# Padding the low part of q and the last value block to 128 rows in a causal attention, mixture-of-experts and dense kernel

## The chip, the cores and the metric

The kernel runs on one core of a Trainium2 chip. The metric is the device time of one execution in microseconds (us). In the profile PE is TensorE's matmul, PEld TensorE's weight load, DVE is VectorE, ACT ScalarE, POOL GpSimd and SP SyncE, which here issues DMAs.

## The reference

Four batches of eight heads (S = 576 positions, D = 64) go through causal attention with a compressive memory; the result, 2304 rows of 512, goes through a top-1 mixture of eight experts and then through a dense layer with a squared ReLU:

```python
scores = np.where(causal, -1000000000.0, scale * np.matmul(q, k.transpose(0, 1, 3, 2)))
a = np.exp(scores - scores.max(-1, keepdims=True))
a /= a.sum(-1, keepdims=True) + 1e-09
local = np.matmul(a, v)
...
x = _moe_ref(x=x, **moe_kwargs)
return _moe2_ref(x=x, **moe2_kwargs)
```

All of it is in float32.

## The kernel before

The attention works on pairs of heads: 16 pairs (b, hp), two heads side by side on 64 partitions each. For precision q/8 and k are each split into a high part in the matmul's own format (qh, kh) and a low part (ql, kl), and a score is qh·kh + qh·kl + ql·kh. For all pairs but the first, the first two products are one matmul with a contraction of 128 rows: SyncE copies, by eight DMAs a pair, qh twice and kh above kl into q2 and k2 (lines 201 and 202). The third product, `product(ql, kh, False, False)` in line 238, takes the 64 partitions of one head, and so its weight load and its matmul stand in the profile as 64\*128 (rows\*columns of the array). After it the causal mask is added by a 128-row matmul with the identity (line 239). `scores` is called for query blocks (3,), then (1, 0), then (2,); each call does both heads one after the other. The last 64 queries of both heads go through `psl` (lines 81 to 83, then 255), whose weights qlast are already 128 rows with zeros (POOL fills them from qh and ql).

A score block is reduced to its negated maximum (DVE, line 244), exponentiated (ACT, line 247), transposed (PE, line 77) and copied to aT (line 159). The product with the values (line 332, pva; line 337, pvb) puts the two heads on 64 columns each (128\*64); its last key block has only LAST = 64 keys and is 64\*64. The result is copied to pvs, transposed (ppt), scaled (DVE, line 350) and joined with the memory's part (POOL, xb).

A pair is a generator that is advanced in four lanes (prep, front, back, end), so that at any time one pair is prepared while another has its scores and a third its product with the values. Inside the attention a scheduler sets each engine's order; the engines then run their lists in order. The pools give each tile its buffers (`bufs`): qh, ql, k2, q2 had two, so a buffer is written again two pairs later. After the attention come the experts (lines 800 on) and the dense layer, in an order written out by hand.

Of the kernel before, what the change touches and what calls it, by code (L numbers as in the profile page):

```python
# [9 lines left out]
F32 = mybir.dt.float32  # L10
F32R = mybir.dt.float32r
# [9 lines left out]
P = 128  # L21
B, H, S, D = 4, 8, 576, 64
# [3 lines left out]
NB = 5  # L26
LAST = S - 4 * P
# [34 lines left out]
NPLAIN = 1  # L62
XB = 2
WARM = 11
MASK_LAST = True
TK = 3
TW = 0
PW = 6
# [67 lines left out]
def attention(tc, c, q, k, v, x_dram, pools):  # L136
    nc = tc.nc
    fr, ld, wk, aw, at, per, lt = pools
# [6 lines left out]
    qpad = [per.tile([P, SP_], F32, name=f"qpad{i}") for i in range(3)]  # L145
    pvs = [lt.tile([P, SP_], F32, name=f"pvs{i}") if i else per.tile([P, SP_], F32, name=f"pvs{i}") for i in range(2)]
    qlast = [[per.tile([P, P], F32R, name=f"qlast{t}{i}") for t in "hl"] for i in range(2)]
    for i in range(3):
        nc.gpsimd.memset(qpad[i][:, S:], 0.0)
    for i in range(2):  # L150
        nc.gpsimd.memset(pvs[i][:, S:], 0.0)
        for t in range(2):
            nc.gpsimd.memset(qlast[i][t].bitcast(F32), 0.0)
    c.setup()
    c.lg = c.pool.tile([P, NCOL, 2 * E], F32, name="lg")
    nc.gpsimd.memset(c.lg, 0.0)
# [4 lines left out]
    def pair(b, hp, lgT):  # L161
        i = (b * (H // 2) + hp) % 2
# [12 lines left out]
        kh = fr.tile([P, S], F32R, tag="kh", name="kh")  # L175
# [2 lines left out]
        early = nc.gpsimd if b or hp > 1 else nc.vector  # L178
        (nc.vector if EV["kl"] == "v" else early).tensor_sub(kl, ks, kh.bitcast(F32))
        yield  # L180
        qh = fr.tile([P, S], F32R, tag="qh", name="qh")
        ql = fr.tile([P, S], F32R, tag="ql", name="ql")
        ex = fr.tile([P, S], F32, tag="ex", name="ex", bufs=1)
        rq = fr.tile([P, S], F32, tag="rq", name="rq", bufs=1)
        nc.scalar.mul(qh, qs, 0.125)
        nc.scalar.activation(ex, qs, AF.Exp)
        nc.scalar.activation(rq, qs, AF.Relu)
        nc.vector.scalar_tensor_tensor(out=ql, in0=qs, scalar=0.125, in1=qh.bitcast(F32), op0=ALU.mult, op1=ALU.subtract)
        for t, src in enumerate((qh, ql)):
            for h in range(2):  # L190
                r = slice(64 * h, 64 * h + 64)
                early.tensor_copy(qlast[i][t][r, r], src[r, 512:S].bitcast(F32))
        stacked = b or hp >= NPLAIN
        if stacked:
            k2 = fr.tile([P, 2, 512], F32R, tag="k2", name="k2")
            q2 = fr.tile([P, 2, 512], F32R, tag="q2", name="q2")
            for h in range(2):
                r = slice(64 * h, 64 * h + 64)
                for g, (kx, n) in enumerate(((kh, 512), (kl, 512))):
                    o = slice(64 * g, 64 * g + 64)  # L200
# [4 lines left out]
            memory_consts(tc, c, per, *c.memory)  # L205
        yield "prep"

        vt = ld.tile([P, NB, 2, D], F32, tag="vraw", name="vraw", bufs=2)
        nc.sync.dma_start(out=vt[:, 0:4].rearrange("p c h d -> p c (h d)"), in_=v[b, hp, 0:512].rearrange("(c p) d -> p c d", p=P))
        nc.sync.dma_start(out=vt[0:LAST, 4].rearrange("p h d -> p (h d)"), in_=v[b, hp, 512:S])  # L210
        negm = wk.tile([P, 2, NB], F32, tag="negm", name="negm")
# [5 lines left out]
        def scores(js):  # L217
            banks = [bank(f"sc{js[0]}{h}") for h in range(2)]
            off = [sum((i + 1) * P for i in js[:t]) for t in range(len(js))]
            o, n = off[-1] + js[-1] * P, len(js)  # L220
            mask = c.maskd.unsqueeze(1).to_broadcast((P, n, P))
            for h in range(2):
                r = slice(64 * h, 64 * h + 64)

                def product(qx, kx, start, stop):
                    for i, j in enumerate(js):
                        nk = (j + 1) * P
                        lhs, rhs = (qx[:, h], kx[:, h]) if len(qx.shape) == 3 else (qx[r], kx[r])
                        nc.tensor.matmul(banks[h][:, off[i]:off[i] + nk], lhsT=lhs[:, j * P:nk], rhs=rhs[:, 0:nk],
                                         start=start and i == 0, stop=stop and i == n - 1)  # L230

                if stacked:
                    product(q2, k2, True, False)
                else:
                    product(qh, kh, True, False)
                    product(qh, kl, False, False)
                if MASK_LAST:
                    product(ql, kh, False, False)
                nc.tensor.matmul(banks[h][:, o - (n - 1) * P:o + P], lhsT=c.identb, rhs=mask, start=False, stop=MASK_LAST)  # L239
                if not MASK_LAST:  # L240
                    product(ql, kh, False, True)
            views = [(banks[h][:, off[i]:off[i] + (j + 1) * P], h, j) for i, j in enumerate(js) for h in range(2)]
            for psv, h, j in views:
                nc.vector.tensor_reduce(out=negm[:, h, j:j + 1], in_=psv, axis=AX.X, op=ALU.max, negate=True)  # L244
            for psv, h, j in views:
                nk = (j + 1) * P
                nc.scalar.activation(a[:, h, aoff[j]:aoff[j] + nk], psv, AF.Exp, bias=negm[:, h, j:j + 1],  # L247
                                     accum_out=ssum[:, h, j:j + 1])
# [10 lines left out]
        nc.gpsimd.tensor_copy(ssum[0:64, 1, 4:5], ssum[64:128, 0, 4:5])  # L259
        yield  # L260
        scores((3,))
        yield
        scores((1, 0))
        yield
        scores((2,))
        yield "front"

        aT = at.tile([P, 2, 1664], F32, tag="aT", name="aT", bufs=2)
        ko = (0, 576, 1024, 1344, 1536)

        def atr(dst, h, kb, j):
# [5 lines left out]
        for k0 in (0, 2):  # L277
            o, st = ko[k0 + 1] - 64, ko[k0 + 2] - ko[k0 + 1]
# [35 lines left out]
        for j0, j1 in ((0, 3), (3, 5)):  # L314
            pm = bank(f"pm{j0}")
            n = j1 - j0
            for j in range(j0, j1):
                nc.tensor.matmul(pm[:, (j - j0) * 130:(j - j0 + 1) * 130], lhsT=qpad[i3][:, j * P:(j + 1) * P], rhs=mb,
                                 start=True, stop=True)
# [5 lines left out]

        pa, pb = bank("pva"), bank("pvb")
        for kb in range(NB):
            kn = P if kb < 4 else LAST
            q0 = max(P, kb * P)
            for h in range(2):  # L330
                o = slice(64 * h, 64 * h + 64)
                nc.tensor.matmul(pa[o, q0 - P:448], lhsT=vt[0:kn, kb, h, :], rhs=aT[0:kn, h, ko[kb] + q0 - kb * P:ko[kb] + S - kb * P],
                                 start=(kb == 0), stop=(kb == NB - 1))
            if kb == 0:
                for h in range(2):
                    o = slice(64 * h, 64 * h + 64)
                    nc.tensor.matmul(pb[o, 0:P], lhsT=vt[:, 0, h, :], rhs=aT[:, h, 0:P], start=True, stop=True)
# [5 lines left out]
        for j0, j1 in ((0, 4), (4, 5)):  # L343
            n = j1 - j0
# [18 lines left out]
        for j0, j1 in ((0, 4), (4, 5)):  # L363
# [3 lines left out]
            n = P if j0 == 0 else 32  # L367
# [41 lines left out]

    order = list(pairs())  # L410
    gens = [pair(*o) for o in order]
    n = len(gens)

# [802 lines left out]
def body(tc, q, k, v, M, z, beta, wg, w1, w2, w_in, w_out, out, dbg=None):  # L1216
# [3 lines left out]
    with ExitStack() as top:  # L1220
# [18 lines left out]
        with ExitStack() as st:  # L1239
            e = st.enter_context  # L1240
            fr = e(tc.tile_pool(name="fr", bufs=2, reuse_waits="tile"))
            aw = e(tc.tile_pool(name="aw", bufs=2, reuse_waits="tile"))
            at = e(tc.tile_pool(name="at", bufs=2, reuse_waits="tile"))
            wk = e(tc.tile_pool(name="wk", bufs=2, reuse_waits="tile"))
            ld = e(tc.tile_pool(name="ld", bufs=4, reuse_waits="tile"))
            per = e(tc.tile_pool(name="per", bufs=1, reuse_waits="tile"))
            c.setup = lambda: (consts(tc, c, per, beta), route_consts(tc, c, rt, x_dram))
            c.memory = (wg, M, z)
            c.route = lambda b: route_batch(tc, c, b, rt)
            c.route_early = route_early(tc, c, cpool, rt)  # L1250
            with tc.manual_schedule(engines=AMAN) if AMAN else nullcontext():
                tail = attention(tc, c, q, k, v, x_dram, (fr, ld, wk, aw, at, per, lt))
            if dbg == "attn":
                for _ in tail:
                    pass
                nc.sync.dma_start(out=out, in_=x_dram[0:N, 0:DM])
                return
# [57 lines left out]
```

## Time and profile before

| what | value |
|---|---|
| median of 3 runs (lowest, highest) | 974.2 us (973.51, 974.49) |
| the profiled execution's own time | 973.51 us |
| its span, first to last instruction | 971.8 us |
| mean granted TensorE clock | 0.986 of full speed |
| PE, DVE, ACT busy over the span | 96%, 62%, 48% |

The profiled execution is the fastest of the three; 1.7 us lie outside its span. A busy PE is not PE at its peak: a matmul counts as busy from its issue to its modelled end, so time in which the array fills or empties is inside the busy time. The attention takes about the first 250 us, the experts up to about 640 us, the dense layer the rest, with the dense weights converted between.

### The profile page before, as it was taken

The numbers are of one execution on the slowest core, as the hardware profiler recorded it, in microseconds if no ns is written. First come the engines' busy times: TensorE is split into PE (matmuls) and PEld (weight loads), VectorE is DVE, ScalarE is ACT, GpSimd is POOL, SyncE is SP. The second block draws the span as 40 slices with busy tenths as digits, with TensorE's granted clock in tenths as the row PEclk, the third lists the DMA queues.
The fourth block names the chain that finished last, engine by engine and source line by source line (L and its number), as shares of the span: only waits on it lengthen the run. The fifth ranks groups of instructions, "written<-read, shape, count | busy, mean of one in ns | idle before, by whom it ended". The sixth has DMA issues, their size and how long they took to land. (4 is left out here: it accounts for less than half of the span.)

```text
span 971.8 us, 14590 instructions
## 1 busy us (share of the span) xinstructions
PE 930.1 (96%) x5212; PEld 735.4 (76%) x5212; DVE 599.5 (62%) x1142; ACT 468.7 (48%) x950; POOL 246.4 (25%) x301
## 2 busy tenths in 40 slices
PE   7999999999999999999999787799999999999996
PEld 4676676776566889889898565678888888888895
DVE  6677878778486887767678899943223222322232
ACT  6877777774445666565563444442222222322231
POOL 6233233231201033054322555562001100100010
PEclk8999999999999999999999999899999999999999
DMA  9675575552746978765735444431000100100000
GB/s 194 168 173 144 145 174 147 131 136 84 236 140 209 377 263 306 258 230 198 272 111 166 136 132 131 130 87 65 12 11 33 33 1 0 44 1 1 12 33 22
DMA packets 80923, 125.03 MB, mean 129 GB/s; under 512 B 8848, under 2 KB 35472, under 8 KB 80848
## 3 DMA queue, kind: packets, MB, share of 16 engines
q1 hardware_dynamic: 76224, 109.11, 37.1%
q0 software_dynamic: 4624, 14.95, 4.8%
q8 instruction: 43, 0.70, 0.3%
q14 instruction: 32, 0.26, 0.1%
HBM read 109.10 MB, written 15.99 MB: 129 GB/s over the span
## 5 line engine op out<-in xcount | busy, mean ns | idle before, releaser
L1165 DVE SCALAR_TENSOR_TENSOR r<-phf,r 128x512 f32<-128x512 f32 (+1 forms) x80 | 50.9, 636 | 178.9 <-ACT r L1164 178.9
L81 PE MATMUL phf<-yT,wi 128*128 128x512 f32 (+1 forms) x320 | 123.3, 385 | 19.2 <-DVE r L1165 19.2
L1164 ACT ACTIVATE r<-phf 128x512 f32<-128x512 f32 (+1 forms) x80 | 44.4, 555 | 177.9 <-PE phf L83 163.0
L848 DVE TENSOR_TENSOR wc<-raw,wc 128x1024 fp32r<-128x1024 f32 x91 | 117.3, 1331 | 12.0 <-ACT wc L846 10.3
L83 PE MATMUL phf<-yT,wi 128*128 128x512 f32 (+1 forms) x320 | 120.1, 375 | 0.0
L82 PE MATMUL phf<-yT,wi 128*128 128x512 f32 (+1 forms) x320 | 119.9, 375 | 0.0
L846 ACT CAST wc<-raw 128x1024 fp32r<-128x1024 f32 x108 | 106.5, 1056 | 20.0 <-DMA raw<-in_w_dram 14.8
L81 PE MATMUL po<-wo,gT 128*128 128x512 f32 x256 | 101.6, 398 | 1.5 <-ACT gT L1167 1.5
L82 PE MATMUL po<-wo,gT 128*128 128x512 f32 x256 | 101.0, 395 | 0.0
L83 PE MATMUL po<-wo,gT 128*128 128x512 f32 x256 | 89.0, 390 | 0.0
L81 PEld LDWEIGHTS phf<-yT,wi 128*128 128x128 f32 x320 | 61.2, 191 | 35.6 <-DVE r L1165 18.6
L244 DVE TENSOR_REDUCE negm<-sc 128x1 f32<-128x512 f32 (+3 forms) x128 | 59.0, 483 | 30.6 <-PE sc L239 28.6
L247 ACT ACTIVATE a<-sc,negm 128x512 f32<-128x512 f32 (+3 forms) x128 | 67.1, 529 | 21.5 <-DVE negm L244 20.7
L81 PE MATMUL py<-wc,hT 128*128 128x512 f32 x176 | 69.9, 397 | 0.7 <-ACT hT L885 0.7
L82 PE MATMUL py<-wc,hT 128*128 128x512 f32 x176 | 68.8, 391 | 0.8 <-DVE wc L848 0.8
L83 PEld LDWEIGHTS phf<-yT,wi 128*128 128x128 f32 x320 | 61.3, 192 | 10.8
L83 PE MATMUL py<-wc,hT 128*128 128x512 f32 x176 | 68.9, 391 | 0.3 <-DVE hT L886 0.3
L82 PEld LDWEIGHTS phf<-yT,wi 128*128 128x128 f32 x320 | 61.5, 192 | 10.0
L848 POOL TENSOR_TENSOR wc<-raw,wc 128x1024 fp32r<-128x1024 f32 x17 | 45.2, 2658 | 91.6 <-ACT wc L846 83.9
L1212 POOL DMA_INDIRECT out_dram<-ob,rtok x13 | 12.9, 991 | 204.7 <-DVE ob L1211 179.6
L1167 ACT CAST gT<-r 128x512 fp32r<-128x512 f32 x64 | 39.8, 621 | 45.4 <-DVE r L1165 37.0
L81 PEld LDWEIGHTS po<-wo,gT 128*128 128x128 f32 x256 | 49.3, 193 | 12.9 <-ACT gT L1167 2.2
(338 smaller groups left out, 2092.5 us busy)
## 6 DMA issues: line engine op xcount, KB each, us to landing
raw<-in_w_dram SPq DMA_DIRECT2D x64, 1024.0 KB, 6.7
fraw<-in_w_in_dram SPq DMA_DIRECT2D x16, 512.0 KB, 4.0
fraw<-in_w_out_dram SPq DMA_DIRECT2D x16, 512.0 KB, 3.7
q<-qh SPq DMA_DIRECT2D x60, 128.0 KB, 2.5
kraw<-in_k_dram SPq DMA_DIRECT2D x16, 288.0 KB, 5.3
qraw<-in_q_dram SPq DMA_DIRECT2D x16, 288.0 KB, 3.2
y_rest<-y SPq DMA_DIRECT2D x17, 256.0 KB, 3.0
vraw<-in_v_dram SPq DMA_DIRECT2D x16, 256.0 KB, 3.1
```

Of the source, the lines that this page charges most:

```text
L81: nc.tensor.matmul(out, lhsT=lh, rhs=rh, start=start, stop=False)
L82: nc.tensor.matmul(out, lhsT=lh, rhs=rl, start=False, stop=False)
L83: return nc.tensor.matmul(out, lhsT=ll, rhs=rh, start=False, stop=stop)
L244: nc.vector.tensor_reduce(out=negm[:, h, j:j + 1], in_=psv, axis=AX.X, op=ALU.max, negate=True)
L247: nc.scalar.activation(a[:, h, aoff[j]:aoff[j] + nk], psv, AF.Exp, bias=negm[:, h, j:j + 1], accum_out=ssum[:, h, j:j + 1])
L846: nc.scalar.copy(wc[:, 0, ks], raw[:, ks])
L848: eng.tensor_sub(wc[:, 1, ks], raw[:, ks], wc[:, 0, ks].bitcast(F32))
L1164: nc.scalar.activation(r[:, 0:nt], ph[:, 0:nt], AF.Relu)
L1165: nc.vector.scalar_tensor_tensor(out=r[:, 0:nt], in0=ph[:, 0:nt], scalar=0.0, in1=r[:, 0:nt], op0=ALU.max, op1=ALU.mult)
L1167: nc.scalar.copy(gT[:, 0, 0:nt], r[:, 0:nt])
L1212: nc.gpsimd.indirect_dma_start(out=out, out_offset=bass.IndirectOffsetOnAxis(ap=c.tok[b0 + j], axis=0), in_=ob, in_offset=None)
```

## The change

The low part of q gets a tile of its own, qlz, of 128 partitions and two head slots; in each slot only one head's 64 partitions are filled, by one DMA a head (two a pair), and the other 64 are zeroed once at the start. The third product takes these 128 rows against all 128 partitions of kh. The mask matmul now always ends the accumulation. The values and aT live in fixed tiles (vts, aTs, two of each) whose last block's rows 64 to 127 are zeroed once, and the product with the values uses 128 rows for the last block too. qh and ql go from two buffers to one.

```diff
+    qlz = [per.tile([P, 2, 512], F32R, name=f"qlz{i}") for i in range(2)]
+    vts = [per.tile([P, NB, 2, D], F32, name=f"vts{i}") for i in range(2)]
+    aTs = [per.tile([P, 2, 1664], F32, name=f"aTs{i}") for i in range(2)]
...
+        for h in range(2):
+            nc.gpsimd.memset(qlz[i][64 - 64 * h:128 - 64 * h, h].bitcast(F32), 0.0)
+        nc.gpsimd.memset(vts[i][LAST:P, 4], 0.0)
+        nc.gpsimd.memset(aTs[i][LAST:P, :, 1536:1600], 0.0)
...
-        qh = fr.tile([P, S], F32R, tag="qh", name="qh")
-        ql = fr.tile([P, S], F32R, tag="ql", name="ql")
+        qh = fr.tile([P, S], F32R, tag="qh", name="qh", bufs=1)
+        ql = fr.tile([P, S], F32R, tag="ql", name="ql", bufs=1)
...
-        for t, src in enumerate((qh, ql)):
-            for h in range(2):
-                r = slice(64 * h, 64 * h + 64)
+        for h in range(2):
+            r = slice(64 * h, 64 * h + 64)
+            nc.sync.dma_start(out=qlz[i][r, h].bitcast(F32), in_=ql[r, 0:512].bitcast(F32))
+            for t, src in enumerate((qh, ql)):
                 early.tensor_copy(qlast[i][t][r, r], src[r, 512:S].bitcast(F32))
...
-        vt = ld.tile([P, NB, 2, D], F32, tag="vraw", name="vraw", bufs=2)
+        vt = vts[i]
...
-                if MASK_LAST:
-                    product(ql, kh, False, False)
-                nc.tensor.matmul(banks[h][:, o - (n - 1) * P:o + P], lhsT=c.identb, rhs=mask, start=False, stop=MASK_LAST)
-                if not MASK_LAST:
-                    product(ql, kh, False, True)
+                for i_, j in enumerate(js):
+                    nk = (j + 1) * P
+                    nc.tensor.matmul(banks[h][:, off[i_]:off[i_] + nk], lhsT=qlz[i][:, h, j * P:nk], rhs=kh[:, 0:nk], start=False, stop=False)
+                nc.tensor.matmul(banks[h][:, o - (n - 1) * P:o + P], lhsT=c.identb, rhs=mask, start=False, stop=True)
...
-        aT = at.tile([P, 2, 1664], F32, tag="aT", name="aT", bufs=2)
+        aT = aTs[i]
...
-            kn = P if kb < 4 else LAST
...
-                nc.tensor.matmul(pa[o, q0 - P:448], lhsT=vt[0:kn, kb, h, :], rhs=aT[0:kn, h, ko[kb] + q0 - kb * P:ko[kb] + S - kb * P],
+                nc.tensor.matmul(pa[o, q0 - P:448], lhsT=vt[:, kb, h, :], rhs=aT[:, h, ko[kb] + q0 - kb * P:ko[kb] + S - kb * P],
```

On PE, in the middle of the attention, the end of one pair's product with the values and the next pair's scores of query block 2 stand like this in the kernel before (sc is the score bank of a head, k and q are the stacked tiles):

```order
L332 MATMUL pva<-aT,vraw 64x192 x2
L337 MATMUL pvb<-aT,vraw 64x128 x2
L332 MATMUL pva<-aT,vraw 64x64 x2
L229 MATMUL sc_1956<-k_1631,q_1632 128x384
L229 MATMUL sc_1956<-kh,ql 128x384
L239 LDWEIGHTS identb
L239 MATMUL sc_1956<-maskd,identb 128x128
```

The same place after the change:

```order
L337 MATMUL pva<-aTs_129,vts_127 64x192 x2
L342 MATMUL pvb<-aTs_129,vts_127 64x128 x2
L337 MATMUL pva<-aTs_129,vts_127 64x64 x2
L236 MATMUL sc_1973<-k_1648,q_1649 128x384
L246 MATMUL sc_1973<-kh,qlz_124 128x384
L247 LDWEIGHTS identb
L247 MATMUL sc_1973<-maskd,identb 128x128
```

No matmul is added or taken away and the order is the same; only the operands of the third product and of the last value block differ.

On SP, one pair's copies in the kernel before, from its loads of the values to the next pair's loads (the numbers tell the buffers of different pairs apart):

```order
L209 DMA vraw_1802<-in_v_dram 128x4x128
L210 DMA vraw_1802<-in_v_dram 64x128
L202 DMA q2_1834<-qh_1821 64x512
L201 DMA k2_1833<-kh_1798 64x512
L202 DMA q2_1834<-qh_1821 64x512
L201 DMA k2_1833<-kl_1800 64x512
L201 DMA k2_1833<-kh_1798 64x512
L202 DMA q2_1834<-qh_1821 64x512
L201 DMA k2_1833<-kl_1800 64x512
L202 DMA q2_1834<-qh_1821 64x512
L360 DMA x_dram_60<-xb_1772 128x4x128
```

And after the change, one pair's copies:

```order
L217 DMA vts1_127<-in_v_dram 64x128
L197 DMA qlz0_124<-ql_2039 64x512 x2
L208 DMA k2_2052<-kh_2016 64x512
L209 DMA q2_2053<-qh_2038 64x512
L208 DMA k2_2052<-kl_2018 64x512
L209 DMA q2_2053<-qh_2038 64x512
L208 DMA k2_2052<-kh_2016 64x512
L209 DMA q2_2053<-qh_2038 64x512
L208 DMA k2_2052<-kl_2018 64x512
L209 DMA q2_2053<-qh_2038 64x512
L365 DMA x_dram_60<-xb_1991 128x4x128
```

The two new copies stand ahead of the eight.

On ACT, the place around the copy of pva in the kernel before; kh_2000 belongs to the pair that is prepared next:

```order
L185 ACTIVATE qh_2225<-qraw_2200 128x576
L186 ACTIVATE ex_2227<-qraw_2200 128x576
L187 ACTIVATE rq_2228<-qraw_2200 128x576
L159 COPY pvs1_119<-pva_1940 128x448
L176 CAST kh_2000<-kraw_1996 128x576
```

The same place after the change, where kh_2016 is that pair's:

```order
L191 ACTIVATE qh_2038<-qraw_2014 128x576
L192 ACTIVATE ex_2242<-qraw_2216 128x576
L193 ACTIVATE rq_2243<-qraw_2216 128x576
L165 COPY pvs1_119<-pva_1957 128x448
L182 CAST kh_2016<-kraw_2012 128x576
```

Before, qh was written for the pair after the one whose kh follows; now qh and kh there belong to the same pair, and ex and rq run one pair ahead of qh.

## Rows read from the trace of the kernel before

**Rows 1.** The page's head: span, then busy time, share, and instructions of each engine.

```profile
span 971.8 us, 14590 instructions
...
PE 930.1 (96%) x5212; PEld 735.4 (76%) x5212; DVE 599.5 (62%) x1142; ACT 468.7 (48%) x950; POOL 246.4 (25%) x301
```

**Rows 2.** Windows: stretch, length, busy PE, PEld, DVE, ACT, POOL; clock, DMA share, GB/s.

```profile
131.70:146.00 14.30, 14.30 (x107) 10.26 (x106) 10.54 (x27) 10.85 (x33) 4.20 (x9) 1.00 0.68 181
...
160.10:175.70 15.60, 15.60 (x119) 11.27 (x118) 14.57 (x49) 10.55 (x28) 4.62 (x9) 1.00 0.64 169
218.50:233.60 15.10, 15.10 (x115) 10.69 (x114) 13.80 (x58) 7.83 (x25) 2.45 (x3) 1.00 0.15 41
233.60:245.50 11.90, 11.29 (x116) 8.19 (x115) 9.67 (x41) 5.47 (x17) 3.75 (x4) 1.00 0.56 198
```

**Rows 3.** Timeline of PE in one pair: start, duration, what, [idle before].

```profile
134.73 0.44 PE L229 MATMUL sc<-k,q 128*128 128x384 f32 x1
135.10 0.44 PE L229 MATMUL sc<-kh,ql 64*128 64x384 f32 x1
...
135.52 0.42 PE L229 MATMUL sc<-k,q 128*128 128x384 f32 x1
...
138.67 0.48 PE L229 MATMUL sc<-k,q 128*128 128x512 f32 x1
139.08 0.49 PE L229 MATMUL sc<-kh,ql 64*128 64x512 f32 x1
...
139.54 0.38 PE L82 MATMUL psl<-kl,qlasth 128*128 128x288 f32 x1
...
142.31 0.43 PE L229 MATMUL sc<-k,q 128*128 128x256 f32 x2
...
143.08 0.42 PE L229 MATMUL sc<-k,q 128*128 128x256 f32 x2
```

**Rows 4.** Timeline of PE's weight loads in the same pair.

```profile
134.47 0.19 PEld L332 LDWEIGHTS pva<-aT,vraw 64*64 64x64 f32 x4 [0.17 <-issue]
...
136.81 0.53 PEld L77 LDWEIGHTS ppt<-ident,pvs 128*128 128x128 f32 x5 [0.25 <-issue]
...
139.08 0.18 PEld L229 LDWEIGHTS sc<-kh,ql 64*128 64x128 f32 x1 [0.25 <-issue]
```

**Rows 5.** Groups by shape, weight loads, 0 to 420 us: busy, mean ns, idle before.

```profile
L229 PEld LDWEIGHTS sc<-kh,ql 64*128 64x128 f32 x128 | 21.3, 184 | 15.8 <-issue 13.1
...
L239 PEld LDWEIGHTS <-identb 128*128 128x128 bf16 x96 | 9.2, 95 | 16.2 <-issue 13.7
```

**Rows 6.** Timeline of PE in the experts, 128-row matmuls in a run.

```profile
349.90 0.39 PE L81 MATMUL py<-wc,hT 128*128 128x512 f32 x1
350.13 0.39 PE L82 MATMUL py<-wc,hT 128*128 128x512 f32 x1
```

**Rows 7.** Timeline of SP's queue in the pair of rows 3.

```profile
134.84 0.38 SPq L209 DMA_DIRECT2D vraw<-in_v_dram  x1
...
139.10 0.60 SPq L201 DMA_DIRECT2D k<-kh  x1
139.74 0.60 SPq L202 DMA_DIRECT2D q<-qh  x1
...
141.20 0.58 SPq L202 DMA_DIRECT2D q<-qh  x1
```

**Rows 8.** The page's DMA issues: count, KB each, median us from issue to landing.

```profile
q<-qh SPq DMA_DIRECT2D x60, 128.0 KB, 2.5
kraw<-in_k_dram SPq DMA_DIRECT2D x16, 288.0 KB, 5.3
```

**Rows 9.** Timeline of ACT around the copy of pva in that pair.

```profile
133.21 0.68 ACT L185 ACTIVATE qh<-qraw 128x576 fp32r<-128x576 f32 x1 [0.41 <-DMA qraw<-in_q_dram]
...
134.95 0.51 ACT L159 COPY pvs<-pva 128x448 f32<-128x448 f32 x1
```

**Rows 10.** Timeline of PE at the start of the attention.

```profile
17.85 1.11 PE L77 MATMUL ptl<-ident,al 128*128 128x128 f32 x4 [5.86 <-ACT al L257]
```

More of the change, by code (lines that the diff above doesn't have):

```diff
@@ L64 @@
 WARM = 11
-MASK_LAST = True
 TK = 3
```

## The prediction

> **What bounds the kernel now.** I read the page's head first: PE is busy for 96% of the span, no other engine above 62% [rows 1]. That share alone settles nothing, because a matmul that waits for the array counts as busy too, so I went to the attention, the only stage the change touches, and cut it at the starts of pva. There are fifteen stretches from one pair's pva to the next. Eleven are like the first of [rows 2], 14.3 us; in these PE is never idle, while DVE works 10.5 us and ACT 10.9. Two are like the second, 15.6 us, where a batch's routing brings DVE to 14.6. The last two rows are the last two stretches, 15.1 and 11.9 us. PE is thus the bound in the eleven, by more than 3 us, and DVE stands close behind it in the others.
>
> What PE does with its time shows when one follows the starts, not the durations. In the experts, 512-column matmuls of 128 rows start 0.23 us apart, though each is shown as 0.39 long [rows 6]. In the scores, the 512-column product of k and q starts at 138.67, the 64-row product with ql at 139.08, 0.41 later, and what stands behind the mask at 139.54 [rows 3]. Nothing waits for data there; the weight load of the 64-row product simply starts 0.25 us after the one before it ended, and "issue" names no releaser [rows 4]. The next weight load, of the mask's identity, idles too. Summed over the attention, PEld was idle 15.8 us ahead of the loads for ql and 16.2 us ahead of the identity's [rows 5]: 32.0 us, 2.0 a pair. So the array does not load the next weights beside a running matmul when the number of rows changes between the two. That is what I take the stall to be; the 128-row neighbours in [rows 6] don't have it.
>
> **The change, part by part.** *The third product at 128 rows.* It takes as many columns as before, so it costs no more streaming. In the order of the changed kernel the scores hold no switch of rows any more, save four at the start, where the first pair's first two products stay at 64 rows. I price it by starts. A head of block 2 (384 columns) takes 135.52 - 134.73 = 0.79 us [rows 3]; without a switch, at 0.23 us per 512 columns [rows 6], two products of 0.17 and a mask of 128 columns at 0.06 make 0.40. That saves 0.39, and 0.78 for two heads. Block 3 takes 0.87 [rows 3] and would take 0.23 + 0.23 + 0.06 = 0.52: 0.35, and 0.70 for two heads. Blocks 1 and 0 together take 0.77 [rows 3]; their 1024 columns would take 0.46, so 0.31 is the most. With four short weight loads in a row I take 0.25, so 0.50 for two heads; nothing and 0.62 are the bounds. Together 1.98 us a pair, which the 2.0 of the idle sums confirms.
>
> *The last value block at 128 rows.* In a usual pair it stands between pvb and the scores. The idle of 0.17 us ahead of its 64\*64 loads [rows 4] goes. A switch of columns stays behind it, from 64 to 128; such a switch has idle as well, 0.25 us ahead of ppt, which comes after a matmul of 32 columns with all 128 rows [rows 4]. I take 0.15 a pair, between 0.1 and 0.3. The Trainium skill, in "TensorEngine Tiling (Array Packing)", Key Properties, says that changing the tiling mode drains the array, without a difference between rows and columns. The row of ppt agrees with it; were it only rows that count, this term would be 0.3 and the sum 1.6 us larger.
>
> *PE in a usual pair* then needs 14.30 - 1.98 - 0.15 = 12.17 us.
>
> *The rest that the pair needs.* ACT has 10.85 and DVE 10.54 us of work [rows 2], which nothing shortens. At 12.17 us ACT would be busy 89% of the time, in a fixed order, behind six score banks; some waits that PE's slowness hid until now will show. Their bounds are nothing and all of the 2.13; I take 0.3, a quarter of the 1.32 us between PE's floor and ACT's work. A usual pair takes 12.45 and saves 1.85: 20.4 us for eleven. In the two stretches of 15.60 DVE's 14.57 is the floor; I take 14.9, 0.7 each, 1.4 together. The stretch of 15.10 has 13.80 of DVE, I take 14.2: 0.9. That of 11.90 holds one score block only, 0.78 + 0.15 at most: 0.7. **Sum: 23.4 us.**
>
> *The two new DMAs and the single qh.* SP issues copies 0.64 us apart [rows 7], so two more cost 1.3 us of its queue a pair. Nobody waits for them soon: their scores come a stretch later. But they stand ahead of the eight copies, and with one qh the next pair's qh may be written only when the last copy of this one has landed. Counted from the end of pva (134.73): the last copy starts at 6.5 now [rows 7], at about 7.2 then, since part of the 1.3 falls into the wait for kl; it lands 2.5 us later [rows 8], at 9.7. Behind qh stand ex, rq and the copy of pva, which starts 1.74 us after qh [rows 9]. So ACT can start the next copy of pva at 11.4, and is wanted at 12.2. The loop is hidden, by 0.8 us. I price it at nothing; what is queued behind qh if the cover goes is ACT's whole list, first the copy of pva for which PE's ppt waits.
>
> *The start.* Eight small memsets on POOL and the way of ql through a DMA delay the first pair's third product by several us. PE stood idle there for 5.9 us anyway, waiting for the exponential of the last queries [rows 10], which needs neither, and the scheduler now puts psl ahead of the third products. I take nothing, with 2 us to either side.
>
> *After the attention* the lists are the same and everything starts from its end, so the gain is carried through. The granted clock in all stretches of [rows 2] is 1.00, that is 2.4 GHz, and I expect no other.
>
> **The sum.** The profiled execution took 973.51 us, the fastest of the runs, whose median is 974.2. 973.51 - 23.4 = 950.1, and I say **950.0**. Its own range is 944 (no loss by coupling: 11 x 2.13 + 2 x 1.03 + 1.3 + 0.93 = 27.7, and 2 at the start) to 956 (0.8 us of coupling a pair instead of 0.3: 11 x 1.33 + 3.0 = 17.6).
>
> **The rivals.** *ACT and DVE take over.* PE gets faster, but the chain from scores to maximum, exponential, transpose and copy sets the pair at 13.2 us or more, since in order both engines already hold 75% of the stretch. For it speaks that both are within 1.7 us of PE's floor [rows 2]; against it that PE had no wait at all before, so there is some distance. With 13.2: 1.1 x 11 + 1.5 = 13.6 saved, 960; from 955 to 967. The Trainium skill warns of this in "TensorEngine Tiling (Array Packing)", PSUM Bottleneck: a faster TensorE leaves the emptying of PSUM as it was. No run here shows yet from where it holds.
>
> *The single qh closes the loop.* If the copies land not after 2.5 but after 5.3 us, as the load of k does [rows 8], the loop is 7.2 + 5.3 + 1.74 = 14.2 us, and with all of the 1.3 on the path 14.7: slower by 0.4 a usual pair, 4.4 for eleven, 978. It decides against the change once the landing exceeds some 5.2 us. Against it: the q copies among these very transfers land in 2.5, and one copy more in five raises the DMA share of 0.68 [rows 2] to less than 0.9 at the shorter pair.
>
> *The rows are not the cause.* If the idle comes with something else that stays, such as loading ql's weights itself, nothing is saved and the two DMAs lie beside: 973.5. Against it, the identity's load idles as much as ql's [rows 5].
>
> *More than the sum.* If the start gains several us from its new order, and coupling costs nothing, 938 to 944.
>
> **How the numbers follow.** Forecast 0.60; ACT and DVE 0.23; more than the sum 0.08; the loop 0.05; not the rows 0.04. From 940 to 962 lies the forecast, some two thirds of the second case and most of the third, a little over 0.8. A difference of 0.2%, about 2 us, is what a measurement of this kernel can tell from no change. Faster: 0.60 + 0.23 + 0.08 and a little of the loop, 0.92; same 0.04; slower 0.04.
>
> **What would show it.** Right: no idle "issue" ahead of the third product's and the mask's weight loads; a head of block 2 at 0.40 us; a usual stretch at 12.2 to 12.8, a routing stretch near 14.9; first waits of PE for ACT and DVE. Wrong in the stall: starts still 0.37 apart. Wrong in the coupling: stretches of 13 us with PE waiting for copies or banks. Wrong in the loop: ACT waiting at qh for the copies of q, more than 1 us each pair.

## The result, and the profile after

The changed kernel takes **950.58 us**, the median of 4 runs (949.08 to 953.61); the kernel before takes 973.89 in the same comparison. The ratio is 0.9764, with a 95% interval from 0.9739 to 0.9789: faster by 23.3 us, where 950.0 was forecast. Its profiled execution took 949.08 us, with this on the page's head (span, then busy time, share and instructions of each engine):

```profile
span 947.3 us, 14682 instructions
...
PE 906.6 (96%) x5212; PEld 730.6 (77%) x5212; DVE 609.4 (64%) x1142; ACT 464.6 (49%) x950; POOL 255.3 (27%) x309
```

PE's share is what it was [rows 1]; the head alone would not show that anything happened. The windows from one pair's pva to the next do (columns as in [rows 2]):

```profile
120.10:132.60 12.50, 12.50 (x109) 9.84 (x108) 11.31 (x26) 10.52 (x32) 4.66 (x9) 1.00 0.83 210
145.10:159.70 14.60, 14.28 (x119) 10.95 (x118) 14.60 (x48) 10.77 (x32) 4.86 (x9) 1.00 0.84 211
197.30:211.20 13.90, 13.43 (x114) 10.29 (x113) 13.53 (x56) 8.07 (x29) 2.47 (x3) 1.00 0.20 57
211.20:222.20 11.00, 10.40 (x114) 8.06 (x113) 9.58 (x42) 5.45 (x17) 3.74 (x4) 1.00 0.57 189
```

A usual stretch went from 14.3 to 12.5 us, and PE is still busy through all of it; a routing stretch from 15.6 to 14.6, and now DVE is the engine that is busy all through. The last pair's pva starts at 222.2 instead of 245.5 us, 23.3 earlier. Of the span's 24.5 us that leaves 1.2 for everything behind. Inside the stretch, PE's timeline (start, duration, what) shows one pair's block 2 and its first head of block 3, to be held against [rows 3]:

```profile
122.69 0.28 PE L337 MATMUL pva<-aTs,vts 128*64 128x64 f32 x4
122.90 0.44 PE L236 MATMUL sc<-k,q 128*128 128x384 f32 x1
123.18 0.34 PE L246 MATMUL sc<-kh,qlz 128*128 128x384 f32 x1
123.36 0.23 PE L247 MATMUL sc<-maskd,identb 128*128 128x128 bf16 x1
123.40 0.42 PE L236 MATMUL sc<-k,q 128*128 128x384 f32 x1
123.66 0.34 PE L246 MATMUL sc<-kh,qlz 128*128 128x384 f32 x1
...
124.00 0.48 PE L377 MATMUL plg<-xTg,wg 128*32 128x160 f32 x8
...
126.26 0.48 PE L236 MATMUL sc<-k,q 128*128 128x512 f32 x1
...
126.86 0.48 PE L236 MATMUL sc<-k,q 128*128 128x512 f32 x1
```

A head of block 2 takes 123.40 - 122.90 = 0.50 us instead of 0.79, one of block 3 0.60 instead of 0.87. The price was 0.40 and 0.52: the starts 0.37 apart are gone, but something of 0.1 us a head was not priced. The weight loads, grouped by shape over 0 to 420 us as in [rows 5], show where idle time is left:

```profile
L246 PEld LDWEIGHTS sc<-kh,qlz 128*128 128x128 f32 x128 | 22.9, 200 | 3.7 <-DMA qlz<-ql 3.7
...
L247 PEld LDWEIGHTS <-identb 128*128 128x128 bf16 x96 | 9.5, 99 | 13.6 <-issue 13.5
```

Ahead of the third product's loads the idle fell from 15.8 to 3.7 us, and those are the start's copies through the DMA. Ahead of the identity's it stayed, at 13.6 of 16.2. At last, the longest waits of PE from 0 to 420 us (total, times, longest):

```profile
PE sc L246 <- DMA qlz<-ql: 2.7, 1, 2.7
PE fperm L605 <- DVE fval L600: 1.5, 1, 1.5
```

No wait of PE recurs with the pair; the largest, for the first pair's copy, stands ahead of the first pva.

### The profile page after: what moved, and what is told of

It is laid out like the page before. It is cut to its first block, busy times and chain, and to the rows that moved or that the text cites. A ratio compares the mean times of both kernels' runs of the same rounds, so it can differ in the third digit from the quotient of the medians.

```text
span 947.3 us, 14682 instructions
## 1 busy us (share of the span) xinstructions
PE 906.6 (96%) x5212; PEld 730.6 (77%) x5212; DVE 609.4 (64%) x1142; ACT 464.6 (49%) x950; POOL 255.3 (27%) x309
## 5 line engine op out<-in xcount | busy, mean ns | idle before, releaser
L853 DVE TENSOR_TENSOR wc<-raw,wc 128x1024 fp32r<-128x1024 f32 x91 | 116.9, 1327 | 12.2 <-ACT wc L851 10.7
L1217 POOL DMA_INDIRECT out_dram<-ob,rtok x13 | 12.9, 991 | 204.7 <-DVE ob L1216 179.6
L250 DVE TENSOR_REDUCE negm<-sc 128x1 f32<-128x512 f32 (+3 forms) x128 | 55.7, 478 | 7.4 <-PE sc L247 7.3
```

The costliest lines, as they stand in the source:

```text
L853: eng.tensor_sub(wc[:, 1, ks], raw[:, ks], wc[:, 0, ks].bitcast(F32))
L1217: nc.gpsimd.indirect_dma_start(out=out, out_offset=bass.IndirectOffsetOnAxis(ap=c.tok[b0 + j], axis=0), in_=ob, in_offset=None)
```

## The experiments

Twelve kernels were run, against the kernel before on the same chips (973.1 to 973.7 us there). "The changed kernel" stands for the 950.6 us.

**The rows alone.** The decisive one: the same copies, buffers and order of instructions, with the third product reading half the rows.

```diff
-  lhsT=qlz[i][:, h, j * P:nk], rhs=kh[:, 0:nk]
+  lhsT=qlz[i][r, h, j * P:nk], rhs=kh[r, 0:nk]
```

> The changed kernel, with one difference: the third product reads 64 rows of the padded tile and of kh instead of 128. The same copies, buffers and order of instructions on TensorE. Switch theory: the scores' 1.6 us of a usual pair come back and nothing else, so the time is that of the run with the padded values alone, 967.8 us (966 to 970), with idle ahead of the third product's and the mask's weight loads. Rival, the copies and the single buffers have a price of their own which shows at this pace: 971 to 977, with ScalarE waiting for copies of q or the load of q. Rival, the padded tile and not its rows makes the gain: 951.

Measured: 969.06 us, ratio 0.9952 (0.9935 to 0.9969). PE's timeline of block 2 in it:

```profile
133.84 0.44 PE L236 MATMUL sc<-k,q 128*128 128x384 f32 x1
134.21 0.44 PE L246 MATMUL sc<-kh,qlz 64*128 64x384 f32 x1
134.58 0.23 PE L247 MATMUL sc<-maskd,identb 128*128 128x128 bf16 x1
134.62 0.42 PE L236 MATMUL sc<-k,q 128*128 128x384 f32 x1
```

Its usual stretch, and the idle ahead of the third product's loads, by window and by group:

```profile
131.00:145.10 14.10, 14.10 (x108) 10.28 (x107) 11.36 (x27) 10.81 (x33) 4.71 (x9) 1.00 0.74 186
```

```profile
L246 PEld LDWEIGHTS sc<-kh,qlz 64*128 64x128 f32 x128 | 21.9, 191 | 20.0 <-issue 11.3 <-DMA qlz<-ql 5.5 <-DMA vts<-in_v_dram 0.5
```

The starts 0.37 apart are back, and the head of 0.78. So 18.5 us of the 23.3 hang on the number of rows and nothing else, 1.6 us a usual pair. The copies and the single buffers show no cost at this pace: the time is within 1.3 us of the next run, which has neither, and the intervals of the two ratios overlap.

This run leaves one other reading open: that a product of 64 rows is slow by itself, whatever stands beside it. The kernel before answers it. All three products of a head of its first pair have 64 rows:

```profile
11.04 0.44 PE L229 MATMUL sc<-kh,qh 64*128 64x384 f32 x1
11.32 0.33 PE L229 MATMUL sc<-kl,qh 64*128 64x384 f32 x1
11.50 0.34 PE L229 MATMUL sc<-kh,ql 64*128 64x384 f32 x1
11.77 0.23 PE L239 MATMUL sc<-maskd,identb 128*128 128x128 bf16 x1
```

The third starts 0.18 us after the second, the distance behind a 128-row product of as many columns in the changed kernel (123.18 to 123.36 above); only the mask, where the rows change, comes 0.27 behind. So it is the change of rows between neighbours that takes the time.

**The values alone**, in the kernel before: fixed tiles, zero rows, 128 rows for the last block.

```diff
-        vt = ld.tile([P, NB, 2, D], F32, tag="vraw", name="vraw", bufs=2)
+        vt = vts[i]
...
-        aT = at.tile([P, 2, 1664], F32, tag="aT", name="aT", bufs=2)
+        aT = aTs[i]
...
-            kn = P if kb < 4 else LAST
```

> The kernel before, with the fixed, zero-padded tiles of values and weights and the last value block at 128 rows; the scores as before. Switch theory: 0.1 to 0.3 us a pair, 971.5 us (969 to 972.5). Rival (the columns, not the rows, or the fixed tiles cost a wait): 973.9 or more.

Measured: 967.76, ratio 0.9946 (0.9928 to 0.9965), 5.9 us and not 2.4. Usual stretches went from 14.28 to 14.13 us as priced, but the routing stretches from 15.70 to 15.20. Why, the weight loads of the kernel before show at the end of pva in a routing stretch:

```profile
162.57 0.19 PEld L332 LDWEIGHTS pva<-aT,vraw 64*64 64x64 f32 x2 [0.28 <-issue]
162.82 0.20 PEld L337 LDWEIGHTS pvb<-aT,vraw 128*64 128x64 f32 x4
163.19 0.19 PEld L332 LDWEIGHTS pva<-aT,vraw 64*64 64x64 f32 x2 [0.17 <-issue]
```

There the last block's heads stand apart, with pvb between them, and the rows change four times instead of twice. From the start of pva to the scores it is 3.40 us in that stretch (160.05 to 163.45) and 2.91 in the same stretch of this run (157.53 to 160.44).

**The scores alone**: the changed kernel with its last value block at 64 rows.

```diff
+            kn = P if kb < 4 else LAST
...
-  lhsT=vt[:, kb, h, :], rhs=aT[:, h, ...
+  lhsT=vt[0:kn, kb, h, :], rhs=aT[0:kn, h, ...
```

> The changed kernel with its last value block at 64 rows again (the zero rows stay, unread). Switch theory: one switch of rows comes back in each of the 16 pairs, 0.15 us each (0.1 to 0.3), 2.4 us in all: 953 us (952 to 955.4), and idle again ahead of the 64*64 weight loads. Rival, only switches of columns count there, which stay either way: 950.6, no difference.

Measured: 954.10, ratio 0.9802 (0.9786 to 0.9817): 3.5 us worse. That interval just overlaps the changed kernel's; the stretches decide. Usual ones take 12.68 us, 0.14 more, the routing ones 15.1 instead of 14.6, and the last pva starts at 226.0 instead of 222.2. Rows do count there.

**The mask's type.** What are the 0.1 us a head? The identity of the mask is bf16 among fp32r weights, and its load still idles.

```diff
+    identr = per.tile([P, P], F32R, name="identr")
+    nc.vector.tensor_copy(identr, c.ident)
+    maskr = per.tile([P, P], F32R, name="maskr")
+    nc.vector.tensor_copy(maskr, c.maskd)
...
-            mask = c.maskd.unsqueeze(1).to_broadcast((P, n, P))
+            mask = maskr.unsqueeze(1).to_broadcast((P, n, P))
...
-  lhsT=c.identb, rhs=mask
+  lhsT=identr, rhs=mask
```

> The changed kernel with the mask's product in the type of the scores (identity and mask as fp32r copies) instead of bf16. In the changed kernel a head of block 2 takes 0.50 us from start to start where its columns need 0.40, and the loss lies between the mask and the next head's third product. Theory A, the switch of type at the mask keeps weight loads from being pulled ahead: 0.08 to 0.1 us a head comes back, 0.5 us for the six heads of a usual pair, 11 x 0.5 = 5.5 and 1 to 2 more at start and end: 944 us (942 to 946); no idle ahead of the identity's loads. Theory B, the loss is three weight loads for three short products, 0.2 us each, whatever the type; an fp32r identity takes 0.2 us to load where the bf16 one takes 0.10: 951 to 957. Theory C, DVE or ACT take over below 12.5 us: PE's starts get closer but the time stays within 2 us of 950.6.

Measured: 951.52, ratio 0.9786 (0.9766 to 0.9807), no difference from the changed kernel. The load of the first head's identity and the starts of its two heads' first products in block 2:

```profile
112.53 0.19 PEld L251 LDWEIGHTS sc<-maskr,identr 128*128 128x128 f32 x1
```

```profile
112.24 0.44 PE L240 MATMUL sc<-k,q 128*128 128x384 f32 x1
...
112.76 0.39 PE L240 MATMUL sc<-k,q 128*128 128x384 f32 x1
```

The idle ahead of the identity is gone, and the head still takes 112.76 - 112.24 = 0.52 us, against 0.50. Theory A falls; idle ahead of a weight load is not by itself lost time.

**Without the mask's product.**

```diff
-  ... start=False, stop=False)
-                nc.tensor.matmul(banks[h][:, o - (n - 1) * P:o + P], lhsT=c.identb, rhs=mask, start=False, stop=True)
+  ... start=False, stop=i_ == n - 1)
```

> The changed kernel without the mask's product in the four full blocks; the triangular mask is left out of the scores there, everything else is computed. Eight products of 1024 columns in all go from a usual pair. If columns alone set TensorE's time, that saves 0.43 us a pair: 12.1 us a stretch, 945 us. If every short product costs its weight load (the identity's transposes stand 0.109 us apart where their 128 columns stream 0.053), it saves 0.8 to 1.0 us a pair: 11.6 us a stretch, 938 to 942 us. If DVE (11.35 us of work) or ScalarE take over first, the stretch stays above 12.1 with waits of TensorE for maxima, exponentials or copies: 944 to 949.

Measured: 954.51, ratio 0.9806 (0.9784 to 0.9828). The whole time can't be read, since other routing changes the stages behind; the last pva starts at 219.5 instead of 222.2. PE's timeline of block 2 and the head of block 3:

```profile
84.50 0.42 PE L236 MATMUL sc<-k,q 128*128 128x384 f32 x1
84.76 0.34 PE L246 MATMUL sc<-kh,qlz 128*128 128x384 f32 x1
84.94 0.35 PE L236 MATMUL sc<-k,q 128*128 128x384 f32 x1
85.12 0.34 PE L246 MATMUL sc<-kh,qlz 128*128 128x384 f32 x1
85.39 0.48 PE L376 MATMUL plg<-xTg,wg 128*32 128x160 f32 x8
```

Behind a third product, the next k,q product is followed after 0.18 us (84.94 to 85.12), its 384 columns' worth. Behind a mask it is followed after 0.26 (123.40 to 123.66 in the changed kernel). The mask itself hands over in 0.04; that its 128 columns are too short to load the weights of the next product beside them is my reading. The block takes 0.89 us instead of 1.10: 0.10 for each mask, where I had priced 0.06. The usual stretches took 11.8 to 12.6 us, 0.7 less at best: more than columns alone would save, less than a whole load each. In the three longest PE was idle for 0.35 us, and in the longest of all ScalarE waited 1.2 us for copies of q.

**The copies twice.**

```diff
+            for _ in range(2):
-            nc.sync.dma_start(out=qlz[i][r, h].bitcast(F32), in_=ql[r, 0:512].bitcast(F32))
+                nc.sync.dma_start(out=qlz[i][r, h].bitcast(F32), in_=ql[r, 0:512].bitcast(F32))
```

> The changed kernel with each of the two copies into the padded tile made twice: 1.3 us more of SP's queue a pair, no other change. The prediction's loop (single qh, ten copies, landing, next qh) had 0.8 us of cover at 12.2 us a pair; in the changed kernel's trace ScalarE already waits 0.3 to 0.4 us for a copy of q in some pairs. Theory, the cover is all but used up: 0.5 to 1.3 us a usual pair, 956 to 966 us, and ScalarE waits at qh for the copies of q. Rival, the copies are hidden by more than 1.3 us: 950.6.

Measured: 972.47, ratio 0.9992 (0.9975 to 1.0008): the whole gain lost. SP's queue, ScalarE and PE in it:

```profile
125.63 1.19 SPq L198 DMA_DIRECT2D qlz<-ql  x2
126.91 0.55 SPq L209 DMA_DIRECT2D k<-kh  x1
128.81 1.10 SPq L198 DMA_DIRECT2D qlz<-ql  x2
129.96 1.64 SPq L210 DMA_DIRECT2D q<-qh  x1
...
134.86 0.59 SPq L210 DMA_DIRECT2D q<-qh  x1
```

```profile
137.38 0.69 ACT L191 ACTIVATE qh<-qraw 128x576 fp32r<-128x576 f32 x1 [1.85 <-DMA q<-qh]
...
139.11 0.51 ACT L165 COPY pvs<-pva 128x448 f32<-128x448 f32 x1
```

```profile
153.87 1.11 PE L76 MATMUL ppt<-ident,pvs 128*128 128x128 f32 x5 [1.68 <-DVE pvs L165]
```

In this pair the prediction's loop is closed: the last copy of qh goes out at 134.86, ScalarE's next qh waits for it until 137.38, ex, rq and the copy of pva stand behind it, and PE waits at ppt. (The row of PE is from the next stretch and names DVE's half of pvs; ScalarE's half, behind a qh that waited 2.97 us, is written at the same time.) The test was coarser than meant. Between the copies SP stood still for 1.35 us, I take it because the repeat writes where the first has not landed. From first to last copy it took 9.2 us (125.63 to 134.86), where the changed kernel takes 5.8 (124.37 to 130.19): 3.4 us more, not 1.3. The 21.9 us are lost unevenly: the first pva starts 2.6 us later than in the changed kernel, the second stretch takes 5.7 more, and three usual stretches take nothing more (12.5). So the run shows the path, and not how much cover was left.

**Copies of q ahead of those of k**, to open that loop, in the changed kernel, with the copies doubled, and without the mask.

```diff
-                    nc.sync.dma_start(out=k2[o, h, 0:n].bitcast(F32), in_=kx[r, 0:n].bitcast(F32))
...
+            for h in range(2):
+                r = slice(64 * h, 64 * h + 64)
+                for g, (kx, n) in enumerate(((kh, 512), (kl, 512))):
+                    o = slice(64 * g, 64 * g + 64)
+                    nc.sync.dma_start(out=k2[o, h, 0:n].bitcast(F32), in_=kx[r, 0:n].bitcast(F32))
```

> The changed kernel with the eight copies that stack k and q in another order: the four of qh stand before the four of k, so the last reader of the single qh is issued 1.9 to 2.6 us earlier. Theory, TensorE sets the usual stretch of the changed kernel (12.54 us, no wait) and the loop over qh only just touches it (ScalarE waits 0.2 to 0.4 us in some pairs): no more wait for q's copies, the same stretch, 950.6 us within 1. Rival, that wait costs the pair something even now: usual stretches below 12.5, 944 to 948.

> The run with each copy into the padded tile made twice, with the four copies of qh ahead of the four of k. Theory, what cost 22 us there is the loop over the single qh (SP's queue up to the last copy of qh, its landing, then ScalarE's next qh, ex, rq and copy of pva): with 1.9 us less queue ahead of that copy the stretches go back to 12.5 to 12.7, 951 to 956 us. Rival, SP's queue as a whole is full (14 issues and waits a pair), so that the loads of the next q and k come late whatever the order: 965 to 973.

> The changed kernel without the mask's product in the four full blocks, which is left out of the scores there, and with the copies of qh ahead of those of k. Without the mask the values and the routing differ, so only the attention's stretches are to be compared. Theory, what held the stretches of the run without the mask at 12.2 us (11.9 to 12.6, where TensorE's own work is 11.8) is the loop over qh and the SP queue: 11.8 us or less here, and ScalarE no longer waits for copies of q. Rival, VectorE and ScalarE hold it (11.3 and 10.6 us of work): again 12.2 us, with waits of TensorE for maxima and exponentials.

Measured: 954.51 (ratio 0.9814, 0.9795 to 0.9833), 974.81 (1.0019, 1.0001 to 1.0036) and 963.31 (0.9893, 0.9876 to 0.9910). None is what the theory said, and none refutes it: the scheduler answered the earlier copies by putting ScalarE's next qh 3 to 4 us earlier too, away from ex and rq and ahead of them, so the distance between copy and qh did not grow. In the second, three of the four copies of qh stayed behind the repeated ones as well, and ScalarE still waited for them, 11.8 us in ten waits between 65 and 200 us. In the third, PE waits for ScalarE's exponentials at 12.56 us a stretch, though it has 12.2 us of work. The edit changed two things, and the size of the cover stays open.

**Other ways to fill the padded tile.** VectorE writes it itself, without copies:

```diff
-        nc.vector.scalar_tensor_tensor(out=ql, in0=qs, scalar=0.125, in1=qh.bitcast(F32), op0=ALU.mult, op1=ALU.subtract)
...
-            nc.sync.dma_start(out=qlz[i][r, h].bitcast(F32), in_=ql[r, 0:512].bitcast(F32))
+            nc.vector.scalar_tensor_tensor(out=qlz[i][r, h], in0=qs[r, 0:512], scalar=0.125, in1=qh[r, 0:512].bitcast(F32), op0=ALU.mult, op1=ALU.subtract)
+        nc.vector.scalar_tensor_tensor(out=ql[:, 512:S], in0=qs[:, 512:S], scalar=0.125, in1=qh[:, 512:S].bitcast(F32), op0=ALU.mult, op1=ALU.subtract)
```

> The changed kernel without the two copies: VectorE writes the low part of q into the padded tile itself, as two operations of 64 partitions x 512 and one of 128x64 in place of one of 128x576. VectorE gets 0.7 to 0.9 us more work a pair (11.35 to 12.1 of 12.54 us in a usual stretch; 14.6 to 15.4 in the two routing stretches, which it bounds); SP's queue gets 1.3 us shorter and the first pair's third product no longer waits for a copy. If the copies cost only at the start: 2 us gained there, 1.5 lost in the routing stretches, 948 to 952. If VectorE takes over: usual stretches of 12.8 or more, 954 to 960. If the copies held the pair up: usual stretches below 12.5.

Measured: 963.25, ratio 0.9898 (0.9877 to 0.9919), usual stretches of 13.5 us. VectorE, in its order:

```profile
133.42 0.68 DVE L196 SCALAR_TENSOR_TENSOR qlz<-qraw,qh 64x512 fp32r<-64x512 f32 x1 [0.36 <-PE sc L248]
134.03 0.54 DVE L252 TENSOR_REDUCE negm<-sc 128x1 f32<-128x384 f32 x1
134.60 0.69 DVE L196 SCALAR_TENSOR_TENSOR qlz<-qraw,qh 64x512 fp32r<-64x512 f32 x1
```

Half the partitions take 0.68 us, nearly the whole 0.79 of ql in one piece, and both stand ahead of the scores' maxima. ScalarE's exponentials wait 18.9 us for maxima between 70 and 200 us, against 9.1 in the changed kernel. VectorE's total (11.6 of 13.5) would not have said so; its place in the order did. Not all of the 12.7 us lies there. In the profiled executions the last pva starts 14.6 us later than in the changed kernel, and 5.8 of these are there before the first pva (34.1 instead of 28.3), behind a wait for the last queries' exponential that the changed kernel does not have:

```profile
21.96 1.11 PE L76 MATMUL ptl<-ident,al 128*128 128x128 f32 x4 [10.52 <-ACT al L265]
```

The stretches cost the other 8.8. And GpSimd, with the copies of q first:

```diff
-            nc.sync.dma_start(out=qlz[i][r, h].bitcast(F32), in_=ql[r, 0:512].bitcast(F32))
+            early.tensor_copy(qlz[i][r, h], ql[r, 0:512].bitcast(F32))
```

> The changed kernel with the copies of qh first and the low part of q put into the padded tile by GpSimd (VectorE for the first pairs), two copies of 64x512 on the same partitions, instead of by DMA. SP's queue is 1.3 us shorter a pair, and the first pair's third product need not wait for a DMA (2.7 us in the changed kernel). GpSimd has 4.7 of 12.5 us busy and gets 2 to 3 more. Theory, the usual stretch stays 12.54 and the start gains 1 to 2.7: 948 to 950. Rival, the copies stand ahead of GpSimd's sums for the output and of kl, which come late then, or VectorE is slowed while GpSimd copies: stretches of 12.8 or more, 954 to 962.

Measured: 953.16, ratio 0.9803 (0.9778 to 0.9828). Most usual stretches stay at 12.5 to 12.9 us and the first is 0.6 shorter, but the first pva starts 2.0 us later, behind a wait of 8.8 us like the one above, and the routing stretches take 15.5 instead of 14.6. By the time alone it is not told apart from the changed kernel.

**The third product at 64 rows from ql itself**, the copies kept but unread:

```diff
-                    nc.tensor.matmul(banks[h][:, off[i_]:off[i_] + nk], lhsT=qlz[i][:, h, j * P:nk], rhs=kh[:, 0:nk], start=False, stop=False)
+                product(ql, kh, False, False)
```

> The changed kernel, but the third product reads ql at 64 rows; the two copies into the padded tile are still made, and nobody reads them; single qh and ql, padded values as in the change. Switch theory: the scores' 1.9 us a pair come back, what stays is the value block's gain: 971.5 us (969 to 973), and the copies and the single buffers cost nothing. Rival, the gain comes from the new order of the program or the buffers: 951 to 960. Rival, the copies have a price that the faster third product pays back: over 974.

Measured: 977.03, ratio 1.0031 (1.0007 to 1.0055), scattered from 970.7 to 984.1, outside the first forecast and where the last rival put it. Its trace is of the fastest execution, 970.7. The run was badly chosen: ql has one buffer, and now TensorE reads it late, so that, as I read it, the next pair's ql, its copies and the loads behind them on SP come late too. ScalarE waited 14.6 us for loads of q between 65 and 200 us; in the changed kernel there is no such wait in that time. The run with the rows alone is the clean form; it shows no such price of the copies.

## Why the prediction was right

**The stall is the change of rows**: shown, by the run with the rows alone for the scores (starts 0.37 apart against 0.28, 0.26 and 0.18, with the same data), by the first pair's three products at 64 rows, and by the run of the scores alone for the values. The Trainium skill, in "TensorEngine Tiling (Array Packing)", Key Properties, has a change of tiling mode drain the array. The starts agree with that, but no run shows the draining itself.

**The sum.** Its terms, against the starts of pva in the traces:

| term | forecast | measured |
|---|---|---|
| scores, a usual pair | 1.98 us | 1.6 (12.54 to 14.11) |
| last value block, a usual pair | 0.15 | 0.15 |
| loss by coupling, a usual pair | 0.3 | 0 in nine of the eleven, where PE is busy all through |
| usual stretch | 12.45 | 12.54 |
| routing stretch | 14.9 | 14.63 |
| stretch of 15.1 | 14.2 | 13.92 |
| last stretch | 11.2 | 11.03 |
| start | 0 | 2.0 gained |

The mechanism was right and two sizes were off, in opposite directions; that 950.0 lies 0.6 us from the result is in part luck. TensorE's floor was put 0.37 too low, since the step "two products of 0.17 and a mask of 128 columns at 0.06 make 0.40" takes each product at its columns. The mask costs 0.10, and the first product of a block 0.28 instead of 0.17 (122.90 to 123.18). The coupling loss that I had put on top did not come, save in the first two stretches. The idle sums, which I took to confirm 1.98 us a pair, do not: 17.3 of their 32.0 us stayed (3.7 and 13.6), so that 0.9 a pair went, while the scores gained 1.6. That PE is never idle in the eleven stretches of before holds for ten; in the first it waits 0.35 us for VectorE. The value block's term held in a usual stretch and was 0.5 instead of 0.15 in a routing stretch, where the order has its rows change twice as often; that is why these beat 14.9 (15.1 without it, in the run of the scores alone). The start gained the 2.0 us that I had only put into the bounds (pva at 28.3 instead of 30.3): the wait of 5.9 us [rows 10] is gone, and one of 2.7 for the first copy through the DMA has come in its place. The two stretches behind it gave nearly as much back, at 13.41 and 13.58 us. In the second of them ScalarE's copy of pva stands behind an ex that waits for the load of q, and PE waits for that copy:

```profile
45.51 0.68 ACT L192 ACTIVATE ex<-qraw 128x576 f32<-128x576 f32 x1 [2.24 <-DMA qraw<-in_q_dram]
```

```profile
47.24 0.66 PE L76 MATMUL ppt<-ident,pvs 128*128 128x128 f32 x4 [0.82 <-ACT pvs L165]
```

**The rivals.** *ACT and DVE take over*: not at 12.54 us. In the routing stretches DVE is busy all through, as forecast, but PE lacks only 0.3 us there, and in the run of the scores alone 0.5 us more of PE's work made them 0.5 us longer; which of the two bounds them is thus not shown. Without the mask, between 11.8 and 12.6 us, waits of PE for ScalarE's exponentials appear; in those orders the point lies there. *The single qh*: right in its path, not in its price. In the changed kernel SP's last copy of qh and ScalarE's next qh stand like this:

```profile
130.19 0.59 SPq L209 DMA_DIRECT2D q<-qh  x1
```

```profile
134.23 0.68 ACT L191 ACTIVATE qh<-qraw 128x576 fp32r<-128x576 f32 x1 [0.35 <-DMA q<-qh]
...
135.97 0.51 ACT L165 COPY pvs<-pva 128x448 f32<-128x448 f32 x1
```

The 7.2 us to the last copy are met (130.19 - 122.9 = 7.3) and the 1.74 behind qh too, but qh could start only 4.0 us after this copy's issue instead of 2.5. ScalarE waits 0.35, and its copy of pva ends 0.5 us ahead of PE's ppt (136.48; ppt starts at 136.96): that is the cover in this pair, where the prediction had 0.8. Four such waits occur, 1.3 us in all, and none shows as a wait of PE. *Not the rows* is refuted. *More than the sum* did not happen: the start gained, but the stretches behind it gave it back.

**Of the signs** I had named, three did not come: the idle ahead of the mask's loads stayed, and in the run with the fp32r mask it went without saving time; a head of block 2 takes 0.50 us and not 0.40; and behind the first two stretches PE waits for neither ACT nor DVE in a usual one.

## What to carry to other kernels

Before trusting a TensorE that is busy all the time, compare the starts of neighbouring matmuls with those of a clean run of the same width; where the number of rows changed between them, 0.1 us went into the 64-row product here and 0.2 out of it (block 2), and zero rows in a tile that is filled off the path bought them back. Price a short product by the starts around it, not by its columns: the mask cost 0.10 us and not 0.06. And count what a pad costs by its place: the same fill showed no cost on a DMA queue for which PE waited only at the start, cost some 9 us in the stretches in front of VectorE's maxima, and twice the fill on that queue cost all of the gain.

## What the runs showed of the hardware that was not expected

DVE's work in a usual stretch rose from 10.5 to 11.3 us, though the change gives it nothing to do. Most of it is one operation of ten columns, cl: 0.26 us on the mean before, 0.85 after. DVE and POOL in one stretch of the changed kernel:

```profile
126.31 1.23 DVE L315 SCALAR_TENSOR_TENSOR cl<-ssum,gneg 128x10 f32<-128x10 f32 x1
```

```profile
126.21 1.71 POOL L357 TENSOR_TENSOR xb<-tl,xm 128x512 f32<-128x512 f32 x2
```

The row of POOL joins two sums, of which the first ends at 127.51; cl ends at 127.53. In nine stretches cl starts 0.1 us behind that first sum and ends with it; where GpSimd is idle, it takes 0.16. So I read it as held, and the profile books that as busy. It comes with the new order of the program and not with the faster pace: in the run with the rows alone, at 14.1 us a stretch, cl takes 1.12 us too. The Trainium skill, in "SBUF — State Buffer", "SBUF: two separate sides", says that VectorE with two inputs from SBUF and GpSimd hold a pair of ports in turn, each for a whole instruction; the 1.23 us agree, but no run here took the two apart.
